# Whole 65-row blocks through DRAM, and weight loads issued by GpSimd, in a delta-rule attention and mixer kernel

## The chip, the cores and the metric

The kernel runs on one core of one Trainium2 chip. The metric is device time in microseconds (us) of the slowest core, so here of the only one. Each execution also has the mean clock granted to TensorE beside it. Timed medians are of repeated executions; stage lengths come from one profiled execution of each kernel, whose span is some 1.8 us shorter than the time of the same execution.

## The reference, cut to what matters

```python
# q, k, v: (4, 8, 768, 48); beta: (4, 8, 768)
for t in range(S):                                  # delta rule, 768 steps
    y[:, :, t] = einsum('bhd,bhde->bhe', q[:, :, t], state)
    v_old = einsum('bhde,bhd->bhe', state, kt)      # kt: normalized k
    state = state + bt * outer(kt, vt - v_old)
x = y.transpose(0, 2, 1, 3).reshape(4, 768, 384)
h  = maximum(x.transpose(0, 2, 1) @ w_tok1, 0) @ w_tok2    # token mixer
u  = x + h.transpose(0, 2, 1)
out = u + maximum(u @ w_ch1, 0) @ w_ch2                    # channel mixer
```

The four weight matrices arrive as 64-bit floats. The kernel takes them apart with integer operations and rounds them itself.

## The kernel before

Time is cut into chunks of 128 steps, six for each of the four sequences, 24 in all. Within a chunk, a 64×64 unit triangular matrix must be inverted for each head and half chunk. The kernel inverts the two 32×32 diagonal blocks of each matrix and makes the rest by matmuls. The inversions of up to four chunks (a "round": two chunks in round 0, four in each later one but the last) are done at once on VectorE, one block in each partition; to get there, masked blocks pass through DRAM and come back with another partition layout, and so does the inverse W.

```python
# prep(u), its end: the four 32x32 quarters of the masked blocks go to DRAM
for par in range(2):
    for i in range(2):
        lo = (4 * j + 2 * par + i) * NB
        row = C * par + HB * i                        # C = 64, HB = 32
        nc.sync.dma_start(
            out=xins[rnd][lo : lo + NB].rearrange("b s t -> s b t"),
            in_=gm[row : row + HB, :, 2, HB * i : HB * i + HB])

# invert(rnd): one block a partition, 60 dependent VectorE instructions
nc.sync.dma_start(out=x, in_=xins.pop(rnd)[0:n])
for s in range(1, HB - 1):
    nc.vector.tensor_tensor(out=tmp, in0=x[...], in1=x[...], op=ALU.mult)   # cut
    nc.vector.tensor_tensor(out=x[...], in0=x[...], in1=tmp, op=ALU.add)    # cut
nc.sync.dma_start(out=w_dram[0:n], in_=x)

# fetch_w(u): four 32-row DMAs bring W of a chunk back    (cut)

# round_weights: one piece of up to 128x384 float64, three VectorE instructions
d64 = loads.tile([128, WP], mybir.dt.int64, name="d64", bufs=3)[:, 0:n]
nc.sync.dma_start(out=d64, in_=src)
...
nc.vector.tensor_scalar(out=f, in0=hi, ...)
nc.vector.scalar_tensor_tensor(out=f, in0=hi, ...)
nc.gpsimd.tensor_tensor(out=f, in0=f, in1=lo, op=ALU.add)
yield
nc.vector.scalar_tensor_tensor(out=dst, in0=a, ..., in1=f.bitcast(FP32), ...)

# the plan: at(time, step, function): a scheduler fixes each engine's order from it
at(-2.7, 2.0 / (HB + 2), invert, 0)
at(-3.9, 0.25, load_weights, (w1, moe_w_tok1), (w2, moe_w_tok2))
at(2.5, 0.3, load_weights, (wc1, moe_w_ch1))
at(6.0, 0.05, load_weights, (wc2, moe_w_ch2))
```

The order of instructions on each engine is fixed when the kernel is built, and each engine works through its own order. An early piece of rounding is therefore done early, whether the engine has time for it or not.

## Time and profile before

| | before |
|---|---|
| time, median (lowest to highest) | 851.56 us (849.85 to 853.35, 4 runs) |
| profiled span, mean granted clock | 850.4 us, 0.924 |
| TensorE (PE) / VectorE (DVE) / GpSimd (POOL) busy | 732.3 / 394.8 / 111.6 us |
| time until TensorE is full | 253 us, in seven stages A to G |
| the rest, H | 597.4 us, of which TensorE is busy 584.1 |

How to read it: TensorE's share is high because H is full. The prediction says what the stages A to G hold, and why the change must act there.

### The profile page before, as it was taken

To read this page: it belongs to the slowest core of one execution; us is meant where nothing else is said; L and a number is where in the kernel's file an instruction comes from. 1 tells how busy PE (TensorE), PEld (TensorE's weight loads), DVE (VectorE), ACT (ScalarE), POOL (GpSimd) and SP (SyncE) were. 2 spreads that over 40 slices of the span, in tenths; PEclk is the share of its full clock that TensorE was granted. 3 is DMA by queue.
4 is the path that set the end of the run, shared out by engine and by line. 5 is a ranking of instruction groups with operands and counts; after the bars stand their busy time and mean duration, and the time that the engine had idled before them with its cause. 6 is when DMAs were issued, how large, how long until landed. Compare 5 with 4: busy or idle time off the path is not lost.

```text
span 850.4 us, 13384 instructions
## 1 busy us (share of the span) xinstructions
PE 732.3 (86%) x5080; PEld 606.6 (71%) x5080; DVE 394.8 (46%) x1081; ACT 253.0 (30%) x596; POOL 111.6 (13%) x142
## 2 busy tenths in 40 slices
PE   5630654969689999999999899999999999999998
PEld 4620644856469797887787888886898888678876
DVE  4487775756973459333267323493229422010000
ACT  5430422744234522333231333311332222111110
POOL 4322112223430211002000001110000000000000
PEclk9765755987899999999999999999999999999999
DMA  7763414445433441224122223202110200000000
GB/s 137 138 144 63 107 28 126 71 82 155 121 109 53 71 94 24 68 44 78 29 48 54 43 49 69 46 19 53 22 39 20 44 11 10 9 1 20 11 9 19
DMA packets 164591, 49.73 MB, mean 58 GB/s; under 512 B 155536, under 2 KB 158608, under 8 KB 164528
## 3 DMA queue, kind: packets, MB, share of 16 engines
q1 hardware_dynamic: 164480, 48.79, 26.6%
q8 instruction: 40, 0.66, 0.3%
q14 instruction: 23, 0.19, 0.1%
q10 hardware_dynamic: 48, 0.10, 0.0%
HBM read 37.85 MB, written 11.01 MB: 57 GB/s over the span
## 4 chain that ended last, share of the span: by engine, by line
PE 49%; DVE 9%; DMA 2%; ACT 2%; issue 1%; SPq 1%; ACTq 0%
PE p_c L549 16%; PE p_o L564 15%; DVE x L377 3%; DVE sub L373 3%; PE p_h L523 3%; PE p_s L482 2%; PE p_g L338 2%; PE p_q L453 2%; PE p L510 2%; PE p_w L470 2%; PE p_x L422 1%; PE p_z L413 1%; SPq L251 1%; PE p_ut L533 1%; DMA kst<-in_k_dram 1%
## 5 line engine op out<-in xcount | busy, mean ns | idle before, releaser
L549 PE MATMUL p_c<-u_t,wc 128*128 128x128 f32 x1728 | 218.2, 280 | 2.5 <-ACT u_t L537 1.8
L549 PEld LDWEIGHTS p_c<-u_t,wc 128*128 128x128 f32 x1728 | 206.5, 195 | 7.8 <-ACT u_t L537 2.5
L564 PE MATMUL p_o<-wc,r 128*128 128x384 f32 x576 | 197.5, 490 | 3.1 <-DVE wc L195 3.1
L564 PEld LDWEIGHTS p_o<-wc,r 128*128 128x128 f32 x576 | 105.0, 191 | 64.8 <-DVE wc L195 4.4
L556 ACT ACTIVATE r<-p_c 128x512 f32<-128x512 f32 x72 | 43.0, 597 | 156.8 <-PE p_c L549 156.4
L373 DVE TENSOR_TENSOR sub<-x 128x84 f32<-128x84 f32 (+22 forms) x210 | 77.3, 368 | 22.9 <-DMA x<-n_dram 18.3
L377 DVE TENSOR_TENSOR x<-x,sub 128x84 f32<-128x84 f32 (+22 forms) x210 | 76.7, 365 | 4.7
L338 PE MATMUL p_g<-kqt,kbd 128*128 128x128 f32 x384 | 60.1, 313 | 17.9 <-ACT kqt L326 17.7
L413 PE MATMUL p_z<-t,gm 128*65 128x64 f32 x384 | 30.7, 236 | 50.2 <-DVE t L407 49.8
L338 PEld LDWEIGHTS p_g<-kqt,kbd 128*128 128x128 f32 x384 | 55.1, 223 | 24.0 <-ACT kqt L326 22.5
L570 DVE TENSOR_TENSOR xb<-xb,p_o 128x384 f32<-128x384 f32 x24 | 13.3, 554 | 116.2 <-PE p_o L564 116.0
L413 PEld LDWEIGHTS p_z<-t,gm 128*65 128x65 f32 x384 | 28.7, 151 | 52.7 <-issue 28.5
L486 DVE TENSOR_TENSOR s_bd<-s_bd,p_s 64x192 f32<-64x192 f32 (+1 forms) x100 | 31.6, 316 | 73.9 <-PE p_s L482 72.2
L482 PE MATMUL p_s<-w_bd,gm 128*128 128x96 f32 x384 | 58.5, 297 | 5.2 <-ACT w_bd L474 4.9
L482 PEld LDWEIGHTS p_s<-w_bd,gm 128*128 128x128 f32 x384 | 52.6, 208 | 10.3 <-ACT w_bd L474 9.1
L340 DVE TENSOR_TENSOR gm<-p_g,mb 128x512 f32<-128x512 f32 x48 | 33.0, 690 | 57.3 <-PE p_g L338 55.0
L453 PE MATMUL p_q<-s_bd,kqt 128*128 128x96 f32 x352 | 50.9, 287 | 4.2 <-DVE s_bd L486 3.9
L453 PEld LDWEIGHTS p_q<-s_bd,kqt 128*128 128x128 f32 x352 | 47.1, 201 | 9.6 <-issue 3.0
L470 PE MATMUL p_w<-r_bd,wt 128*65 128x96 f32 x384 | 45.5, 263 | 7.2 <-issue 3.5
L455 DVE TENSOR_TENSOR r_bd<-v_st,p_q 64x192 f32<-64x192 f32 (+1 forms) x110 | 34.8, 316 | 35.1 <-PE p_q L453 23.0
L459 ACT ACTIVATE xb<-p_q 64x384 f32<-64x384 f32 (+1 forms) x55 | 23.0, 419 | 92.7 <-DVE r_bd L455 92.4
L474 ACT COPY w_bd<-p_w 64x192 f32<-64x192 f32 (+1 forms) x120 | 33.5, 280 | 54.0 <-PE p_w L470 52.0
(70 smaller groups left out, 708.8 us busy)
## 6 DMA issues: line engine op xcount, KB each, us to landing
d<-in_moe_w_ch_dram SPq DMA_DIRECT2D x24, 384.0 KB, 3.3
kpad<-in_k_dram SPq DMA_DIRECT2D x24, 192.0 KB, 3.5
kst<-in_k_dram SPq DMA_DIRECT2D x96, 48.0 KB, 2.6
qpad<-in_q_dram SPq DMA_DIRECT2D x24, 192.0 KB, 3.6
v_st<-in_v_dram SPq DMA_DIRECT2D x96, 48.0 KB, 2.6
out_dram<-xb SPq DMA_DIRECT2D x24, 192.0 KB, 1.9
n_dram<-gm SPq DMA_DIRECT2D x96, 32.0 KB, 1.7
wt<-w_dram SPq DMA_DIRECT2D x96, 32.0 KB, 2.1
```

The lines of the kernel that those rows point to most:

```text
L338: nc.tensor.matmul(p_g[:, i], kbd[:, nb], kqt[:, nb])
L373: nc.vector.tensor_tensor(out=tmp, in0=x[:, 0:s, s : s + 1].to_broadcast([n, s, w]), in1=x[:, s : s + 1, s + 1 : HB].to_broadcast([n, s, w ...
L377: nc.vector.tensor_tensor(out=x[:, 0:s, s + 1 : HB], in0=x[:, 0:s, s + 1 : HB], in1=tmp, op=ALU.add,)
L413: nc.tensor.matmul(p_z[0:65, nb], gm[:, lo : lo + 65], t11[:, nb])
L453: nc.tensor.matmul(p_q[:, p], kqt[:, 2 * p + cc], s0[:, p])
L455: nc.vector.tensor_tensor(out=r_bd[r, hp, e], in0=v_st[r, hp, cc], in1=p_q[hi, hp, e], op=ALU.subtract,)
L470: nc.tensor.matmul(p_w[0 : C + 1, p], wts[u % NW][:, w_lo : w_lo + C + 1], r_bd[:, p])
L474: nc.scalar.copy(w_bd[r, hp, e], p_w[lo, hp, e])
L482: nc.tensor.matmul(p_s[:, p], gm[:, 2 * p + cc, 0:2], w_bd[:, p])
L549: nc.tensor.matmul(p_c[:, i], wc1[:, cb, f * 128 : (f + 1) * 128], u_t[:, cb], start=(cb == 0), stop=(cb == NCB - 1),)
L556: nc.scalar.activation(r, p_c, ACTF.Relu)
L564: nc.tensor.matmul(p_o, r2[f // FG][:, f % FG], wc2[:, f], start=(f == 0), stop=(f == NHT - 1),)
```

## The change

The intent: fewer and longer transfers on the sync queue. The masked blocks are stored whole (64×64, with one spare row each, 65 rows of pitch). At that pitch the second diagonal 32×32 block lies exactly half a pitch after the first, so one strided transfer takes all diagonal blocks of a round. W is fetched as whole blocks, which needs zeros in the other quarters, so the two W buffers are cleared once. The 34 weight loads leave the sync queue for GpSimd. Smaller parts: three `kst` buffers and not two, the square in place, and some shifted plan times.

```diff
-        nc.sync.dma_start(out=d64, in_=src)
+        nc.gpsimd.dma_start(out=d64, in_=src)
...
-        nc.scalar.square(a, hi.bitcast(FP32))
+        a = hi.bitcast(FP32)                       # after both uses of hi
+        nc.scalar.square(a, a)
...
+    BP = C * C + C
+    def clear_w(i):                                # zeros over one W buffer
+        nc.gpsimd.dma_start(out=w_drams[i]..., in_=z.to_broadcast([128, n, 520]))
+    def diagonal(t, n):
+        t = t[0 : n * BP // 2].rearrange("(b x) -> b x", x=BP // 2)
+        return t[:, 0 : HB * C].rearrange("b (s t) -> b s t", t=C)[:, :, 0:HB]
...
-        ksts[u] = kst = loads.tile([128, NP, 2, D], FP32, name="kst")
+        ksts[u] = kst = loads.tile([128, NP, 2, D], FP32, name="kst", bufs=NK)
...
-        (four stores of 32-row quarters)
+            nc.sync.dma_start(out=rows(n_drams[rnd % 2], j, par), in_=gm[r, :, 2])
...
-        nc.sync.dma_start(out=x, in_=xins.pop(rnd)[0:n])
+        nc.sync.dma_start(out=x, in_=diagonal(n_drams[rnd % 2], n))
...
-        nc.sync.dma_start(out=w_dram[0:n], in_=x)
+        nc.sync.dma_start(out=diagonal(w_drams[rnd % 2], n), in_=x)
...
-        (four fetches of 32-row quarters)
+            nc.sync.dma_start(out=wt_of(u)[r], in_=rows(w_drams[rnd % 2], j, par))
...
+    for i in range(2):
+        at(-3.0 + i, 0, clear_w, i)
-                at(-2.7 + 0.4 * j, 0.06, prep, u)      # round 1
+                at(-3.0 + 0.4 * j, 0.06, prep, u)
-            at(-2.7, 2.0 / (HB + 2), invert, rnd)      # round 0
+            at(-2.5, 2.0 / (HB + 2), invert, rnd)
```

More of the change, by code (lines that the diff above doesn't have):

```diff
@@ L181, in round_weights @@
         f = loads.tile([128, WP], U32, name="w_f")[:, 0:n]
-        a = loads.tile([128, WP], FP32, name="w_a")[:, 0:n]
         nc.scalar.activation(lo, lo, ACTF.Copy, scale=2.0**-29)
-        nc.scalar.square(a, hi.bitcast(FP32))
         nc.vector.tensor_scalar(
@@ L218, with rows @@
     ksts = {}
-    xins = {}
-    xouts = {}
+    BP = C * C + C
+    n_drams, w_drams = [
+        [dram.tile([RU * 2 * NB * BP], FP32, name=f"{name}{i}") for i in range(2)]
+        for name in ("n_dram", "w_dram")
+    ]
+    def clear_w(i):
+        z = zst[:, None, 0:520]
+        n = w_drams[i].shape[0] // (128 * 520)
+        nc.gpsimd.dma_start(
+            out=w_drams[i].rearrange("(p n x) -> p n x", p=128, x=520),
+            in_=z.to_broadcast([128, n, 520]),
+        )
+    def diagonal(t, n):
+        t = t[0 : n * BP // 2].rearrange("(b x) -> b x", x=BP // 2)
+        return t[:, 0 : HB * C].rearrange("b (s t) -> b s t", t=C)[:, :, 0:HB]
+    def rows(t, j, par):
+        lo = (2 * j + par) * NB * BP
+        t = t[lo : lo + NB * BP].rearrange("(b x) -> b x", x=BP)
+        return t[:, 0 : C * C].rearrange("b (s t) -> s b t", t=C)
     rounds = [[0, 1], [2, 3, 4, 5]]
@@ L349, in prep @@
         rnd, j = round_of[u]
-        if j == 0:
-            xins[rnd] = dram.tile([RU * 4 * NB, HB, HB], FP32, name="n_dram")
         for par in range(2):
-            for i in range(2):
-                lo = (4 * j + 2 * par + i) * NB
-                row = C * par + HB * i
-                nc.sync.dma_start(
-                    out=xins[rnd][lo : lo + NB].rearrange("b s t -> s b t"),
-                    in_=gm[row : row + HB, :, 2, HB * i : HB * i + HB],
-                )
+            r = slice(C * par, C * par + C)
+            nc.sync.dma_start(out=rows(n_drams[rnd % 2], j, par), in_=gm[r, :, 2])
         yield
@@ L382, in invert @@
         nc.vector.memset(x.rearrange("b s t -> b (s t)")[:, 0 :: HB + 1], 1.0)
-        xouts[rnd] = w_dram = dram.tile([RU * 4 * NB, HB, HB], FP32, name="w_dram")
-        nc.sync.dma_start(out=w_dram[0:n], in_=x)
+        nc.sync.dma_start(out=diagonal(w_drams[rnd % 2], n), in_=x)
         yield
@@ L389, in fetch_w @@
         rnd, j = round_of[u]
-        w_dram, wt = xouts[rnd], wt_of(u)
-        for i in range(2):
-            for par in range(2):
-                lo = (4 * j + 2 * par + i) * NB
-                row = C * par + HB * i
-                nc.sync.dma_start(
-                    out=wt[row : row + HB, :, HB * i : HB * i + HB],
-                    in_=w_dram[lo : lo + NB].rearrange("b s t -> s b t"),
-                )
+        for par in range(2):
+            r = slice(C * par, C * par + C)
+            nc.sync.dma_start(out=wt_of(u)[r], in_=rows(w_drams[rnd % 2], j, par))
     def join(u):
@@ L602, in start @@
         return u if b == 0 else NCH * b + 0.4 + c * (NCH - 0.5) / NCH
-    for u in range(NK):
+    at(-9.5, 0, load_kq, 0)
+    at(-9.4, 5.6, load_beta)
+    for u in range(1, NK):
         at(-9 + 0.1 * u, 0, load_kq, u)
-    at(-8.95, 4, load_beta)
+    for i in range(2):
+        at(-3.0 + i, 0, clear_w, i)
     for rnd, us in enumerate(rounds):
@@ L610 @@
             if rnd == 0:
-                at(-3.5 + 0.3 * j, 0.06, prep, u)
+                at(-3.7 + 0.3 * j, 0.06, prep, u)
             elif rnd == 1:
-                at(-2.7 + 0.4 * j, 0.06, prep, u)
+                at(-3.0 + 0.4 * j, 0.06, prep, u)
             else:
```

## The prediction

> **What bounds the kernel now.** I read the page first, then cut the span into stages and asked for busy time by engine in each, then the same for the weight-rounding tile alone, then the timelines of VectorE, TensorE and the DMA queue at the seams.
>
> ```profile
> PE 732.3 (86%) x5080; PEld 606.6 (71%) x5080; DVE 394.8 (46%) x1081; ACT 253.0 (30%) x596; POOL 111.6 (13%) x142
> ...
> PE   5630654969689999999999899999999999999998
> ...
> PEclk9765755987899999999999999999999999999999
> ```
>
> TensorE is full from the twelfth slice (about 253 us) to the end. Before that it is half idle and its clock sags. The change can pay only in the first 253 us, unless it makes new holes later. The stages (bounds from the timeline: VectorE's first and last step of the first two triangular inversions, first matmul of the first mixer, TensorE full):
>
> ```profile
> core 0: us, PE busy (x) PEld busy (x) DVE busy (x) ACT busy (x) POOL busy (x), PEclk, DMA share, GB/s
> ...
> 8.60:48.40 39.80, 25.36 (x124) 22.32 (x124) 19.70 (x54) 21.61 (x48) 13.88 (x16) 0.79 0.76 145
> 48.40:78.70 30.30, 3.71 (x16) 3.48 (x16) 28.95 (x83) 5.60 (x12) 6.09 (x7) 0.58 0.47 96
> 78.70:87.80 9.10, 2.01 (x17) 1.88 (x17) 2.66 (x7) 0.93 (x3) 3.00 (x6) 0.50 0.64 136
> 87.80:131.40 43.60, 23.34 (x144) 20.26 (x144) 35.54 (x117) 14.70 (x44) 8.24 (x8) 0.62 0.27 67
> 131.40:139.30 7.90, 0.03 (x1) 0.03 (x1) 6.21 (x18) 2.05 (x5) 3.17 (x3) 0.50 0.57 133
> 139.30:202.20 62.90, 51.16 (x408) 47.03 (x409) 35.54 (x109) 32.22 (x92) 12.01 (x13) 0.80 0.46 97
> 202.20:253.00 50.80, 38.78 (x155) 25.32 (x155) 44.85 (x120) 17.51 (x37) 20.90 (x20) 0.90 0.40 120
> 253.00:850.40 597.40, 584.11 (x4169) 482.92 (x4167) 218.76 (x566) 156.53 (x353) 38.27 (x45) 1.00 0.18 38
> ```
>
> I call them A (preparing the masked blocks), B (inversion of round 0), C (its trip through DRAM), D (inversion of round 1, with the recurrence of round 0 between its steps), E (trip of round 1), F (recurrence of round 1), G (first mixer) and H. They are one chain: x has one buffer, so D cannot load before B has written out; F needs D's W; G needs F's rows. VectorE bounds B (28.95 of 30.30) and G (44.85 of 50.80). H has 13.3 us of TensorE idle; the rest of it is matmul.
>
> Weight rounding alone, by stage (columns: stage, VectorE, GpSimd, clock, DMA):
>
> ```profile
> 48.40:78.70 30.30, 5.29 (x13) 4.01 (x4) 0.58 0.47 96
> ...
> 139.30:202.20 62.90, 4.71 (x10) 3.53 (x4) 0.80 0.46 97
> 202.20:253.00 50.80, 23.35 (x44) 17.50 (x15) 0.90 0.40 120
> ```
>
> So 44 of the 102 VectorE rounding instructions (34 pieces of three) lie in G, which they make VectorE-bound.
>
> **What the Trainium skill says.** SBUF — State Buffer, section Who interferes with whom: a VectorE instruction with two SBUF inputs contends with a GpSimd one that reads SBUF, and the later one blocks. The trace agrees. GpSimd's rounding add runs at 65.72 for 1.00, and the inversion step issued after it takes three times its usual 0.39:
>
> ```profile
> 65.42 0.39 DVE L373 TENSOR_TENSOR sub<-x 64x234 f32<-64x234 f32 x1
> 65.83 1.14 DVE L377 TENSOR_TENSOR x<-x,sub 64x234 f32<-64x234 f32 x1
> ```
>
> Each piece rounded inside an inversion thus costs VectorE its three slots (0.27+0.47+0.47 us from start to start at 384 columns) and about 0.75 us of blocking. DMA: Bandwidth & Descriptors, section Issuing engines are not separate DMA queues: another issuing engine saves only sequencer time. In section Latency and other measured facts it gives the GpSimd path about 1 us to the first byte against 0.6; no run of before shows it, GpSimd issues nothing there. Its section Why small descriptors are slow has a fixed cost per piece. The trace agrees:
>
> ```profile
> kpad<-in_k_dram SPq DMA_DIRECT2D x24, 192.0 KB, 3.5
> kst<-in_k_dram SPq DMA_DIRECT2D x96, 48.0 KB, 2.6
> ...
> x<-n_dram SPq DMA_DIRECT2D x5, 512.0 KB, 4.3
> w_dram<-x SPq DMA_DIRECT2D x5, 512.0 KB, 2.6
> ```
>
> kpad is 1024 runs of 192 bytes, 64 for each of 16 engines, kst 256, 16 each: 0.9 us over 48 runs is 19 ns a run.
>
> **The change part by part.**
>
> *Queue.* n_dram and wt go from 96 issues each to 48 (runs of 256 bytes in place of 128); 34 weight loads leave the queue. That is 130 issues of 0.33 to 0.5 us, some 55 us of queue time over the span. It matters in A, where the queue issues almost without a pause to 67 us. The read of x for round 0, issued at 34.86, should go out near 29: six sets of k and q at 4 us, three stores of 1.1, from 0.74 on. But VectorE starts B only at 48.37, behind other work, so those 6 us are no gain by themselves. Three kst buffers and not two take a 3 us wait (180.8 to 183.9) off the queue in F, just ahead of the W load that TensorE waits 6.24 us for at 190.7.
>
> *DRAM trips.* x was 4 KB runs; it becomes 32 rows of 128 bytes out of a 256-byte pitch: 4096 runs, 256 an engine. At 19 ns the load goes from 4.3 to about 2.3+4.9 = 7 us; the store from 2.6 to about 6, or 4 for round 0, which is half. wt stays near 2.5.
>
> *Order.* This I take from the order of instructions in the two builds. With weight loads on a queue of their own, weights arrive early and the scheduler puts their rounding wherever it sees VectorE room. VectorE rounding instructions: ahead of B 18 before, 36 after; between B's steps 11 and 39; in C 1 and 20; in D 11 and 7; in F 17 and 0; from the next inversion on 44 and 0. So G is freed, but the work goes into B, the other stage that VectorE bounds. B also now starts behind the blocks of all six chunks, not five.
>
> *Extra transfers.* Two clears of w_dram at 1.06 MB, in A or near it, where DMA is already at 0.76; at the 145 GB/s seen there each is about 7 us of all engines, though nothing needs them before B's end.
>
> Stage by stage (after minus before, us):
> - A: a chunk's preparation repeats each 6.4 us (VectorE's second mask product at 23.06, 29.55, 35.83). Six chunks end near 16.9+5*6.4 = 49, plus the four rounding slots before B; GpSimd now has 12 adds, 14 issues at about 1 us (estimate from the page's first-byte figure) and the mask products, close to all of A. I take a start at 54: +5.5.
> - B: its own 60 steps are 21 us alone. Something between each step hides about 0.1 us of dependence, so some 16.5. 39 slots at 0.40 are 15.7, 13 blockings at 0.75 are 10, the other small ones 2.3: 45 with a little waiting 46. The same sum for before is 18.3+4.4+3+3 = 29, measured 30.3. Change +16.
> - C: store 4, W of the first chunk 1, load 7, waits: 13 to 15, with seven pieces in it, each limited by three buffers (issue 1, landing 3.3, rounding 2.5, so 7 us for three, 2.3 a piece, 16 for seven). I take 14.5: +5.5.
> - D: four fewer slots, W further ahead: -2.5.
> - E: +1.
> - F: 17 slots (6.8 us) gone, about half on its path, and half of the W wait: -7.
> - G: 44 rounding instructions gone. What remains on VectorE is about 22 us, so TensorE bounds it: 38.8 busy, a little less at a better clock, plus 3 of waits, 41: -10.
> - H: same matmuls; 3 us longer each way for x and W in five rounds against a freer queue: 0 to +3.
>
> Sum 5.5+16+5.5-2.5+1-7-10+1 = +9.5. A shorter G and a better-fed F would look like success; B pays for them.
>
> **The rivals.** (1) *The weights ride free in A to C and only G's gain counts.* Speaking for it: B's steps depend on each other, so a slot between them hides 0.1 us, and the queue in A is relieved. Against: B is at 96% VectorE already. It would give 851-17-3 = about 831. (2) *GpSimd becomes the brake:* issue, clears and adds in one in-order engine; the mask products of A stand behind loads that wait for a buffer held until the last rounding step (the square is now in place in d64). If each issue costs 2 us and not 1, A and B lose another 10 to 15: 870 to 878. (3) *The finer runs of x open holes in H:* five rounds at up to 6 us, 865 to 880; against it, TensorE has mixer matmuls to fill most of them: in H it idles only 13.3 us though each round's trip takes some 6 us.
>
> **Range and chances.** The sum gives 861. The savings in F and G are surer than the loss in A, where I may be too pessimistic, so I go down to 857. Rival 1 sets the lower side, 2 and 3 the upper: 841 to 875. Faster by 2% needs under 834.5: 0.12. Slower by 2% needs over 868.5: 0.22.
>
> **What would show it.** B's first to last step about 46 us with rounding steps between (under 35: wrong). D starting near 112 to 115 and not 87.8. No rounding in G, and G near 41. The x load near 7 us. GpSimd busy time rising only by its issues. H with 13 to 17 us of TensorE idle. The prediction is wrong if rounding beside an inversion costs under 1 us a piece, or if GpSimd's issues take several us.

## The result, and the profile after

| | before | after |
|---|---|---|
| time, median (lowest to highest) | 851.56 us (849.85 to 853.35) | 876.83 us (875.47 to 878.46, 4 runs) |
| profiled span, clock | 850.4 us, 0.924 | 873.7 us, 0.904 |

The ratio is 1.030 (95% interval 1.027 to 1.033): slower by 3%. Ratios here are of fast runs in the same rounds, so they are not quite the ratio of the medians quoted. Where two experiments are compared that ran in different rounds, I subtract their ratios to before and multiply by 851.5 us; each ratio has an interval of about ±0.3%, that is ±2.5 us, and the difference of two about ±3.5 us.

The page of after begins as follows: busy time by engine, then the busy tenths of TensorE, its granted clock and DMA in 40 slices.

```profile
PE 727.5 (83%) x5080; PEld 604.4 (69%) x5080; DVE 397.2 (45%) x1081; ACT 255.8 (29%) x596; POOL 131.1 (15%) x178
...
PE   5620016369699999999999999999999999999998
...
PEclk9755556569699999999999999999999999999999
DMA  9995281235513543233231414223111200000000
```

The amounts of work are almost those of before. GpSimd has 36 more entries and 20 us more (34 issues and two clears, some 0.56 us each). But slices 4 to 6, roughly 66 to 131 us, hold almost no TensorE work, and its clock falls to half there. DMA is full for the first three slices. The same row of before:

```profile
DMA  7763414445433441224122223202110200000000
```

The stages of after, cut at the same events, A to H (window, then its length, then busy time and count of PE, PEld, DVE, ACT and POOL, granted clock, DMA share and rate):

```profile
8.60:61.02 52.42, 28.23 (x140) 24.11 (x140) 33.35 (x78) 28.26 (x63) 30.56 (x38) 0.73 1.06 242
61.02:108.79 47.77, 0.00 (x0) 0.00 (x0) 46.39 (x113) 16.26 (x33) 26.77 (x34) 0.50 0.46 124
108.79:127.36 18.57, 1.62 (x15) 1.66 (x16) 10.95 (x22) 6.17 (x12) 9.58 (x13) 0.50 0.87 180
127.36:171.43 44.07, 25.28 (x148) 21.93 (x146) 34.41 (x118) 13.76 (x43) 6.85 (x8) 0.58 0.16 35
171.43:181.11 9.68, 0.00 (x0) 0.00 (x0) 0.87 (x2) 0.00 (x0) 0.00 (x0) 0.50 0.61 112
181.11:242.04 60.93, 51.42 (x408) 47.44 (x409) 31.55 (x103) 27.71 (x83) 9.75 (x12) 0.81 0.47 81
242.04:276.25 34.21, 33.64 (x151) 22.59 (x150) 23.73 (x73) 4.85 (x10) 1.73 (x2) 0.97 0.23 41
276.25:873.70 597.45, 583.51 (x4171) 483.26 (x4170) 212.77 (x564) 156.26 (x352) 38.63 (x45) 1.00 0.22 44
```

Lengths against the fence of stages in the prediction: A +12.6, B +17.5, C +9.5, D +0.5, E +1.8, F −2.0, G −16.6, H 0.0; together +23.3, the difference of the spans. The time was lost before the first inversion's trip through DRAM was over (A to C, +39.6) and only part of it came back in G. In B, VectorE is busy 46.39 of 47.77 us with 113 instructions, where before had 83. The weight-rounding tile alone, in A, B and C of after (columns VectorE, GpSimd, clock, DMA share, GB/s), shows what the extra instructions are:

```profile
8.60:61.02 52.42, 21.37 (x36) 10.52 (x12) 0.73 1.06 242
61.02:108.79 47.77, 23.43 (x41) 14.18 (x13) 0.50 0.46 124
108.79:127.36 18.57, 10.18 (x20) 6.37 (x6) 0.50 0.87 180
```

(The 41 of B include two that touch its edges; 39 lie between its steps.) In G the tile no longer appears. The timeline of VectorE in B of after shows how the two kinds of work alternate (start, duration, engine, line, operation):

```profile
62.15 0.20 DVE L392 TENSOR_TENSOR sub<-x 64x58 f32<-64x58 f32 x1
62.39 1.25 DVE L396 TENSOR_TENSOR x<-x,sub 64x58 f32<-64x58 f32 x1
63.57 0.34 DVE L183 TENSOR_SCALAR w_f<-d 128x384 uint32<-128x384 uint32 x1
63.84 0.23 DVE L392 TENSOR_TENSOR sub<-x 64x84 f32<-64x84 f32 x1
63.99 0.55 DVE L187 SCALAR_TENSOR_TENSOR w_f<-d,w_f 128x384 uint32<-128x384 uint32 x1
64.46 0.23 DVE L396 TENSOR_TENSOR x<-x,sub 64x84 f32<-64x84 f32 x1
```

A rounding step stands between two steps of an inversion again and again, and one `x<-x,sub` of 58 columns takes 1.25 us where its neighbour of 84 columns takes 0.23. GpSimd's rounding add runs at the same moment:

```profile
62.53 1.03 POOL L193 TENSOR_TENSOR w_f<-w_f,d 128x384 uint32<-128x384 uint32 x1
```

Each of the 13 adds in B overlaps one VectorE instruction that is stretched, to between 0.8 and 1.4 us; six of these are rounding steps themselves. In 11 of the 13 the stretched one had started after the add, as the prediction says. In two, this one among them, it had started up to 0.14 us before, so the start times alone do not decide who waits.

The transfers concerned, after, in the view of DMA issues (count, KB each, median us from issue to landing):

```profile
d<-in_moe_w_ch_dram POOLq DMA_DIRECT2D x24, 384.0 KB, 3.8
n_dram<-gm SPq DMA_DIRECT2D x48, 128.0 KB, 2.7
wt<-w_dram SPq DMA_DIRECT2D x48, 128.0 KB, 3.4
x<-n_dram SPq DMA_DIRECT2D x5, 512.0 KB, 6.0
w_dram<-x SPq DMA_DIRECT2D x5, 512.0 KB, 5.0
```

The x load went from 4.3 to 6.0 us and its store from 2.6 to 5.0 (before's in the prediction). The stores of masked blocks took 1.7 us before and now 2.7, the W fetches 2.1 and now 3.4: half as many, each with four times the bytes and twice the rows.

### The profile page after: what moved, and what is told of

The parts are those of the page before. It is cut to its first block, busy times and chain, and to the rows that moved or that the text cites. A ratio compares the mean times of both kernels' runs of the same rounds, so it can differ in the third digit from the quotient of the medians.

```text
span 873.7 us, 13277 instructions
## 1 busy us (share of the span) xinstructions
PE 727.5 (83%) x5080; PEld 604.4 (69%) x5080; DVE 397.2 (45%) x1081; ACT 255.8 (29%) x596; POOL 131.1 (15%) x178
## 5 line engine op out<-in xcount | busy, mean ns | idle before, releaser
L561 PE MATMUL p_c<-u_t,wc 128*128 128x128 f32 x1728 | 214.7, 277 | 1.2 <-ACT u_t L549 1.1
L561 PEld LDWEIGHTS p_c<-u_t,wc 128*128 128x128 f32 x1728 | 203.0, 192 | 5.0 <-ACT u_t L549 1.8
L576 PE MATMUL p_o<-wc,r 128*128 128x384 f32 x576 | 194.9, 487 | 0.0
L425 PE MATMUL p_z<-t,gm 128*65 128x64 f32 x384 | 32.6, 243 | 96.3 <-DVE t L419 96.3
L392 DVE TENSOR_TENSOR sub<-x 128x84 f32<-128x84 f32 (+22 forms) x210 | 75.9, 362 | 22.6 <-DMA x<-n_dram 17.6
L396 DVE TENSOR_TENSOR x<-x,sub 128x84 f32<-128x84 f32 (+22 forms) x210 | 74.6, 355 | 4.6
L364 PE MATMUL p_g<-kqt,kbd 128*128 128x128 f32 x384 | 58.6, 307 | 15.3 <-ACT kqt L352 15.2
L582 DVE TENSOR_TENSOR xb<-xb,p_o 128x384 f32<-128x384 f32 x24 | 13.3, 554 | 119.8 <-PE p_o L576 119.6
L364 PEld LDWEIGHTS p_g<-kqt,kbd 128*128 128x128 f32 x384 | 53.5, 217 | 20.4 <-ACT kqt L352 18.6
L465 PEld LDWEIGHTS p_q<-s_bd,kqt 128*128 128x128 f32 x352 | 47.9, 203 | 11.2 <-PE p_q L465 2.4
L353 POOL TENSOR_TENSOR gm<-kst,cs 128x384 f32<-128x384 f32 x24 | 21.1, 877 | 215.3 <-PE p_s L494 173.3
L482 PE MATMUL p_w<-r_bd,wt 128*65 128x96 f32 x384 | 45.3, 262 | 7.7 <-DVE r_bd L467 5.7
```

The source lines that it names most:

```text
L364: nc.tensor.matmul(p_g[:, i], kbd[:, nb], kqt[:, nb])
L392: nc.vector.tensor_tensor(out=tmp, in0=x[:, 0:s, s : s + 1].to_broadcast([n, s, w]), in1=x[:, s : s + 1, s + 1 : HB].to_broadcast([n, s, w ...
L396: nc.vector.tensor_tensor(out=x[:, 0:s, s + 1 : HB], in0=x[:, 0:s, s + 1 : HB], in1=tmp, op=ALU.add,)
L425: nc.tensor.matmul(p_z[0:65, nb], gm[:, lo : lo + 65], t11[:, nb])
L465: nc.tensor.matmul(p_q[:, p], kqt[:, 2 * p + cc], s0[:, p])
L482: nc.tensor.matmul(p_w[0 : C + 1, p], wts[u % NW][:, w_lo : w_lo + C + 1], r_bd[:, p])
```

## The experiments

My theory after reading the traces: the one word `gpsimd` costs most of it, through the order. Weights arrive early, their rounding goes into the stage that VectorE bounds, and it costs more there than it saves in G. Rivals: the DRAM layout and its extra traffic; GpSimd as a brake.

Stage lengths of all runs in us, with the VectorE rounding instructions in A / B / C / D / E and F together / G and later, and the ratio to before. The last two counts are parted at the first step of the next inversion, a few instructions before the end of F:

| run | ratio | A | B | C | D | E | F | G | H | rounding |
|---|---|---|---|---|---|---|---|---|---|---|
| before | 1 | 39.8 | 30.3 | 9.1 | 43.6 | 7.9 | 62.9 | 50.8 | 597.4 | 18/11/1/11/17/44 |
| after | 1.0297 | 52.4 | 47.8 | 18.6 | 44.1 | 9.7 | 60.9 | 34.2 | 597.5 | 36/39/20/7/0/0 |
| e1 after, sync weights | 1.0040 | 45.0 | 27.0 | 11.5 | 44.2 | 10.6 | 61.8 | 48.7 | 596.4 | 18/9/3/8/20/44 |
| e2 before, GpSimd weights | 1.0122 | 40.3 | 52.8 | 15.3 | 41.6 | 5.6 | 61.8 | 39.7 | 593.8 | 33/44/18/7/0/0 |
| e3 after, no clear, quarter fetch | 1.0221 | 53.6 | 45.8 | 18.4 | 40.8 | 8.5 | 60.8 | 34.7 | 595.5 | 40/38/21/3/0/0 |
| e4 after, gated | 1.0055 | 46.1 | 22.6 | 13.4 | 40.0 | 9.7 | 74.4 | 40.6 | 597.2 | 30/0/2/1/36/33 |
| e5 after, no GpSimd add | 1.0113 | 46.9 | 41.2 | 18.5 | 42.0 | 9.4 | 61.2 | 34.4 | 596.8 | 38/39/21/4/0/0 |
| e6 before, small parts | 0.9970 | 45.6 | 27.1 | 8.9 | 46.2 | 7.2 | 61.4 | 52.7 | 591.4 | 18/9/3/11/15/46 |
| e7 before, gated | 0.9891 | 37.0 | 25.3 | 11.4 | 40.9 | 5.4 | 70.2 | 40.6 | 604.6 | 30/0/2/1/41/28 |
| e8 before, gated a round later | 0.9905 | 37.7 | 25.4 | 9.0 | 39.5 | 5.4 | 72.7 | 41.6 | 601.0 | 30/0/0/0/49/23 |
| e9 e6 + GpSimd weights | 1.0104 | 47.8 | 47.9 | 15.1 | 45.3 | 5.6 | 56.8 | 39.6 | 590.7 | 37/39/16/10/0/0 |
| e10 e9 + gate | 0.9879 | 45.5 | 22.6 | 11.4 | 40.1 | 5.6 | 69.4 | 40.5 | 598.5 | 30/0/2/1/36/33 |
| e11 e3 with the clears | 1.0251 | 53.6 | 47.7 | 18.6 | 42.8 | 8.2 | 60.8 | 33.9 | 596.4 | 36/39/20/7/0/0 |
| e12 e4, no clear, quarter fetch | 0.9994 | 44.3 | 22.7 | 15.7 | 39.0 | 8.5 | 73.2 | 40.6 | 596.8 | 30/0/3/0/37/32 |

G begins with the first mixer matmul and ends with the first 24 output matmuls. As other work is mixed in on both sides, a few us can move across these borders, so F, G and H are also read as a sum. Each row of stages is one execution, and those of a kernel differ by 1 to 8 us (e7 and e10, among others, were profiled in their slowest, 846.0 and 844.1).

**e1: the one word undone, in after.**

```diff
-        nc.gpsimd.dma_start(out=d64, in_=src)
+        nc.sync.dma_start(out=d64, in_=src)
```

> The changed kernel with one word put back: the weight pieces are issued by the sync queue again. In the build this returns the rounding to where it was (18, 9, 3, 8, 20, 44 of the 102 instructions in A, B, C, D, F and later). Theory 1, the early rounding is what costs: A to C shrink to near the old lengths (B 30 us, not 47.8) and the time falls to 846 to 858. Theory 2, the whole-block DRAM traffic (clears, 128-byte runs) is what costs: B shrinks, but A stays above 48 and the trips long, and the time stays at 866 or more.

Measured: 854.62 us, ratio 1.0040 (1.0014 to 1.0066). Some 22 of the 25 us are gone. The window of B, with 9 rounding instructions left in it:

```profile
53.65:80.68 27.03, 0.00 (x0) 0.00 (x0) 25.41 (x74) 3.79 (x8) 3.03 (x3) 0.52 0.33 68
```

So with the weights on the sync queue everything else in the change costs little.

**e2: that word alone, in before.**

```diff
-        nc.sync.dma_start(out=d64, in_=src)
+        nc.gpsimd.dma_start(out=d64, in_=src)
```

> The kernel before with that one word changed alone: weight pieces issued by GpSimd, all DRAM traffic as before, no clears. The build has 33, 44, 18, 7, 0, 0 rounding instructions by stage. Theory 1: 864 to 878, B near 48, C near 15 to 18. Theory 2: 846 to 856. If the two causes add, about 866, with A several us shorter than in the changed kernel since there are no clears.

Measured: 861.09 us, ratio 1.0122 (1.0093 to 1.0151). The trace shows the prediction's pattern in full: 44 rounding instructions inside B, none from E on, B +22.5, C +6.2, G −11.1.

```profile
48.93:101.76 52.83, 3.58 (x16) 3.40 (x16) 49.80 (x124) 17.90 (x38) 33.06 (x39) 0.53 0.63 152
```

The time lies between the two forecasts, below the first theory's 864. The word alone costs about 10 us, yet undoing it in after gains 22. The two parts of the change do not add, and e6 and e9 to e12 look for the difference.

**e3: after without the clears, W fetched by quarters.**

```diff
-    for i in range(2):
-        at(-3.0 + i, 0, clear_w, i)
...
-            nc.sync.dma_start(out=wt_of(u)[r], in_=rows(w_drams[rnd % 2], j, par))
+            for i in range(2):                     # src = rows(...), row = C*par + HB*i
+                e = slice(HB * i, HB * i + HB)
+                nc.sync.dma_start(out=wt[row : row + HB, :, e], in_=src[e, :, e])
```

> The changed kernel without the two clears: W's 32-row quarters alone are fetched out of the pitched blocks (96 issues again), weights still by GpSimd. If the clears fill the DMA engines in A and so delay it, A falls from 52.4 to about 45 and the time to 866 to 870. If A is long only because of the rounding in it, the time stays within 2 us of 876.8. B stays near 47 in both.

Measured: 868.65 us, ratio 1.0221 (1.018 to 1.0262), 0.76% or 6.5 us better than after. A did not shorten (53.6), against the thought that the clears crowd it; the time came out as that thought had it, so the forecast was missed in part.

**e4: after, with the 24 channel-weight pieces held back.** A one-element copy on GpSimd, which reads the first W of round 0 once it is back, stands ahead of the first three loads; the rest queue behind.

```diff
+        if gate is not None:                       # gate = lambda: wts[0]
+            nc.gpsimd.tensor_copy(out=d64.bitcast(FP32)[0:1, 0:1], in_=gate()[0:1, 0:1])
         nc.gpsimd.dma_start(out=d64, in_=src)
```

> The changed kernel, the 24 channel weight pieces held back until the first W is joined (a one-element copy ahead of the first three loads), still issued by GpSimd. The build has 30, 0, 2, 1, 36, 33 rounding instructions by stage. Theory 1: B falls to about 25 us and C to 10 to 13, A to about 47 to 50, F a little longer, time 835 to 852. If it is GpSimd's way of issuing that costs, and not the order, the time stays above 865.

Measured: 855.59 us, ratio 1.0055 (1.003 to 1.008). That is 3.6 us above the forecast's 852. The run keeps GpSimd issue and the layout, and moves the 24 loads with their rounding. Its B and its F:

```profile
54.69:77.29 22.60, 0.00 (x0) 0.00 (x0) 20.67 (x66) 1.14 (x3) 2.51 (x5) 0.55 0.21 38
...
140.37:214.81 74.44, 52.54 (x409) 47.85 (x409) 54.36 (x141) 41.76 (x112) 32.02 (x42) 0.78 0.64 146
```

B without any rounding is 22.6 us, so in after each of the 39 instructions cost (47.8 − 22.6)/39 = 0.65 us. This is an upper figure: B of after has 47 VectorE instructions more (113 against 66), and over all of them it is 0.54. The gate takes the loads' own traffic out of B as well; but VectorE is busy there for 46.39 of 47.77 us in after, and waits less than 1 us for weights. F took 36 (with E; 39 up to its end) and grew by (74.4 − 60.9)/36 = 0.37 us for each. From before to after, F and G together lost 61 of them and 18.6 us, 0.30 each, the layout's part in F and G included. An instruction moved from there into B therefore costs 0.54 to 0.65 and saves 0.3 to 0.4. This shows the exchange of the prediction, with its rates.

**e5: after without GpSimd's rounding add.** The add was taken out, so the last bits of the low word are lost.

```diff
-        nc.gpsimd.tensor_tensor(out=f, in0=f, in1=lo, op=ALU.add)
```

> The changed kernel without GpSimd's rounding add, so that the low bits of the weights are cut off (wrong in the last place on purpose). The order keeps 38, 39, 21, 4, 0, 0 rounding instructions by stage, so all of VectorE's slots stay where they are. If blocking by GpSimd's reads is 0.75 us a piece as predicted, B falls by 13 x 0.75 = 10 us to about 38, A and C by some 4 each as there is no add to wait for, and the time to 856 to 864. If the early rounding costs its VectorE slots alone, B stays above 45 and the time above 870.

Measured: 860.83 us, ratio 1.0113 (1.0086 to 1.0141), some 16 us better than after, with nearly the same order (39 instructions in B). Its B:

```profile
55.46:96.68 41.22, 0.00 (x0) 0.00 (x0) 37.07 (x112) 16.27 (x33) 12.50 (x21) 0.51 0.60 164
```

B fell by 6.6 us, 0.5 us for each of 13 adds (10 had been expected), and A by 5.6; C did not fall. VectorE's busy time in B fell by 9.3 us with one instruction fewer, 0.72 for each add, so the loss lay inside its instructions; the rest returned as waits. Removing the add also frees GpSimd, and the order ahead of B is another one, without the wait of 3.67 us that is shown further down, so not all of the 16 us is blocking.

**e6: only the small parts, in before** (plan times of after, three `kst` buffers, square in place).

```diff
-            at(-2.7, 2.0 / (HB + 2), invert, rnd)
+            at(-2.5, 2.0 / (HB + 2), invert, rnd)      # and the other plan times
+        ... name="kst", bufs=NK)    a = hi.bitcast(FP32); nc.scalar.square(a, a)
```

> The kernel before with only the small parts of the change: new plan times, three kst buffers, the square in place; weights on the sync queue, DRAM traffic as before. The weights-on-sync version of the changed kernel measured 854.62, 3.4 us over before. If that was the finer DRAM runs (C and E longer by 2.4 and 2.7), this one is at 848 to 853 with E near 8 and C near 9. If the later start of B (A 45 and not 39.8) was from the plan times, A is again near 44 to 45, and it may be at 854.

Measured: 848.81 us, ratio 0.9970 (0.994 to 0.9999). A grows by 5.8 (more chunks are prepared ahead of B), B, F and H shrink. A long A is not itself a loss if the work it holds is taken from later stages.

**e7 and e8: before with GpSimd loads and the gate**, on the first W of round 0 (e7) or of round 1 (e8: `wts[2]`).

```diff
-        nc.sync.dma_start(out=d64, in_=src)
+        if gate is not None:                       # e7: wts[0]    e8: wts[2]
+            nc.gpsimd.tensor_copy(out=d64.bitcast(FP32)[0:1, 0:1], in_=gate()[0:1, 0:1])
+        nc.gpsimd.dma_start(out=d64, in_=src)
```

> The kernel before, weights issued by GpSimd, the 24 channel pieces held back until the first W is joined; DRAM traffic as before. 30, 0, 2, 1, 41, 28 rounding instructions by stage. Like the gated version of the changed kernel (A 46.1, B 22.6, C 13.4, D 40.0, E 9.7, F 74.4, G 40.6) but with the short trips and with A as in the version with GpSimd's issue alone (40.3, two mask products left to B): A 41, B 25, C 10, D 40, E 6 to 7, F 74, G 40, H 595: about 841 to 847, faster than before. If the finer runs cost nothing, it equals 855.6.

> The same with the pieces held back until the first W of round 1 is joined, so that D and E hold no rounding at all: 30, 0, 0, 0, 49, 23. Rounding in F costs about 0.37 us an instruction (74.4 against 60.9 with 36 of them), so F about 78 and G 38: 839 to 848, within 3 us of the other gate. If rounding in F beyond what VectorE has free there delays the recurrence more than that, F exceeds 82 and the time 850.

Measured: 841.36 us, ratio 0.9891 (0.985 to 0.9932), and 842.88 us, 0.9905 (0.9881 to 0.9929). With the rounding kept out of B, GpSimd issue turns from a loss of 1.2% into a gain of 1%. Where in F it lands makes no difference that these runs resolve.

**e9: small parts and GpSimd issue together, in before.**

```diff
+        (e6, and)
-        nc.sync.dma_start(out=d64, in_=src)
+        nc.gpsimd.dma_start(out=d64, in_=src)
```

> The kernel before with GpSimd's issue and the small parts (plan times, three kst buffers, square in place), DRAM traffic as before. Apart they measured +9.9 and -2.4, so 858 to 860 if they add. The changed kernel measured 876.8; if it is the DRAM traffic together with GpSimd's early loads that fills the DMA engines in A, this one stays at 858 to 862 with A plus B near 93. If instead the plan times with the early rounding make A long (B behind six chunks), it is at 868 or more with A plus B near 99.

Measured: 859.73 us, ratio 1.0104 (1.0067 to 1.0141). They simply add (−0.3% and +1.2% against +1.0%), so the missing piece between e9 and after, 1.93% or 16.4 us, belongs to the DRAM layout. By stages, after minus e9: A +4.6, C and E +7.6, F, G and H together +5.5, B and D −1.3; sum 16.4 (from the table's rounded lengths; the spans differ by 16.3). A and B together take 95.8, where 93 had been expected.

**e10: e9 with the gate** (e9's diff and e7's gate on `wts[0]`).

```diff
+        (e9, and) nc.gpsimd.tensor_copy(out=d64..., in_=wts[0][0:1, 0:1]) ahead of the first 3 loads
```

> The gated kernel of 841.36 (pieces held back until the first W is joined, DRAM as before) with the small parts added. 30, 0, 2, 1, 36, 33 rounding instructions by stage, the same as the gated changed kernel at 855.59. If the small parts are worth their 2.4 here too: 838 to 840. The distance to 855.59 is then the DRAM change alone, in a kernel whose order is the same: 14 to 18 if it costs as much as beside early weights, 6 as with weights on the sync queue.

Measured: 840.04 us (839.58 to 844.1), ratio 0.9879 (0.9848 to 0.9911): the fastest median here, and it beats both kernels, with the old layout. Against e9 only the place of the 24 loads and their rounding differs: 2.25%, 19 us. From after to e4 the same gate gave 2.42%. Its E and F:

```profile
128.24:133.81 5.57, 0.00 (x0) 0.00 (x0) 0.87 (x3) 0.00 (x0) 0.00 (x0) 0.50 0.38 118
133.81:203.22 69.41, 51.18 (x409) 46.69 (x409) 50.81 (x138) 41.08 (x110) 31.72 (x40) 0.80 0.60 142
```

e4 has the same places for the rounding and the new layout: its E is 9.7 and its F 74.4. The ratios put the layout at 1.76%, 15.0 us, here (10.3 between the two profiled executions, which are e4's fastest and e10's slowest). With sync weights (e1 against e6) it is 0.70%, 6.0 us.

**e11: e3 with the clears put back**, which parts them from the fetch.

```diff
+    for i in range(2):
+        at(-3.0 + i, 0, clear_w, i)
```

> The changed kernel with the clears but the quarter fetch of W (the version without either measured 868.65, the changed kernel 876.83). If the clears cost the 8 us, this one is at 875 to 878; if fetching W as whole blocks costs them, it is at 867 to 870.

Measured: 872.80 us, ratio 1.0251 (1.0223 to 1.0278), between the two forecasts. Clears +0.30% (2.6 us) and whole-block fetch +0.46% (3.9 us), each within the error of such a difference; together the 6.5 us of e3.

**e12: e4 without clears, W by quarters** (e3's diff on e4).

```diff
-        at(-3.0 + i, 0, clear_w, i)
+        (quarter fetch as in e3)
```

> The gated changed kernel took 855.6 us and the gated kernel with the old DRAM layout 840.0, so the layout costs 15.6 us here. This run takes the two clears away and fetches W by 32-row quarters again, and keeps the 65-row pitch and the diagonal transfers of x. In the ungated form the clears were worth 4.1 us and the whole-block fetch 4.0. If these two simply add: 847 us (845 to 850), trip E near 8.3 us in place of 9.7, and the recurrence F shorter by some 2 of its 5 extra us. If instead the layout's cost lies in the diagonal runs alone, and the clears only hurt where weight loads crowd them in the first stage: 852 to 856. If clears and fetch explain it all: 840 to 843.

Measured: 850.66 us, ratio 0.9994 (0.9967 to 1.0021), just past the first theory's 845 to 850 and below the second's 852. Clears and fetch are worth 0.61% or 5.2 us here, like the 6.5 ungated. What then remains of the layout (whole-block stores, diagonal transfers of x) is 1.15%, 9.8 us, against 1.17%, 10.0 us ungated (e3 against e9). So two thirds of its cost beside GpSimd loads lies in these, in both orders. The medians in the issue view give the trip of round 1 some 5 us more (load 1.7, store 2.4, the stores ahead of it 1.0) and that of round 0, at half the size, some 3 (load 4.7 and 5.5, store 2.9 and 4.1, the stores ahead 1.0). This estimate of 8 us comes near the 10, and was not tested by itself.

## Why the prediction was right or wrong

The direction, the mechanism and the pattern of stages were right; the size was not. 876.8 lies just above the range (841 to 875). Its sum was +9.5; the spans differ by +23.3. Here each term meets its stage. The way from before to after by e6 (small parts), e9 (and GpSimd issue) and after (and the layout) tells the cause.

- **B, +16: right (+17.5).** Own steps 22.6 and not 21. For a rounded piece the prediction had three slots of 0.40 and 0.75 of blocking, 1.95 us; measured 3 × 0.65 = 1.94, which has the other small instructions in it that the prediction counted apart (2.3 us). So near a match is in part luck. Blocking took 0.72 us an add of VectorE's busy time (e5), as said; only 0.5 of it came off the stage when the add went.
- **A, +5.5: failed (+12.6).** The six chunks ahead of B were named, and e6 shows them: +5.8, all of what was predicted. On top come +2.2 with GpSimd's issues and +4.6 with the layout, which the prediction put at nothing there. Most of the 4.6 is one wait. VectorE starts a like rounding step at 56.12 in after and at 56.16 in e9. In e9 the first step of the inversion comes next:

```profile
56.16 0.35 DVE L183 TENSOR_SCALAR w_f<-d 128x384 uint32<-128x384 uint32 x1
56.43 0.18 DVE L373 TENSOR_TENSOR sub<-x 64x30 f32<-64x30 f32 x1
```

In the built order of after one more rounding step stands ahead of it, and VectorE waits 3.67 us for that step's weights:

```profile
56.51 0.56 DVE L187 SCALAR_TENSOR_TENSOR w_f<-d,w_f 128x384 uint32<-128x384 uint32 x1
60.74 0.36 DVE L183 TENSOR_SCALAR w_f<-d 128x384 uint32<-128x384 uint32 x1 [3.67 <-DMA d<-in_moe_w_ch_dram]
61.02 0.17 DVE L392 TENSOR_TENSOR sub<-x 64x30 f32<-64x30 f32 x1
```

GpSimd issued the load waited for at 55.33. In e9 the load issued at 55.37 is met between two inversion steps, with a wait of 0.69 us. e3 and e11, whose A is 53.6, have the wait ahead of B too, 2.67 and 2.43 us. In e4 and e10 the last mask product stands just ahead of B and no weights do, and the layout's part in A is +0.6. No run took the wait away by itself. The read of x, expected near 29 us, went out at 36.43 (before 34.86), with DMA full in A (share 1.06, before 0.76) and the four `kst` issues of a chunk at 2.6 to 4.6 us (2.6 to 3.4 before); but it was issued 24 us before B began and did not set A's end.
- **C, +5.5: half the size (+9.5).** GpSimd issue gives +6.2 of it, as 16 to 20 rounding instructions fall into the stage, and the layout +3.5. The lengths of the transfers were near: 4 for the store and 7 for the load, and in C of after they took 4.5 and 7.3. But they do not set its end. The load, issued at 114.59, had landed by 121.9, and D's first step came at 127.36, behind rounding steps of which one waited 3.08 us for its weights. That is the prediction's other sum (16 for seven pieces), from which it went down to 14.5.
- **D, −2.5: wrong (+0.5), as a sum of two.** Four rounding instructions fewer are worth what was said: e2 has 7 in D and 41.6 us, before 11 and 43.6. The plan times, left out of this term, lengthen it (e6, 11 and 46.2); after with its 7 has 44.1.
- **E, +1: right (+1.8), as a sum of two.** Without rounding in it and with the old layout E is 5.6; the layout adds 4.1.
- **F, −7, and G, −10: right in the sum (−17; measured −18.6), wrong in the split (−2.0 and −16.6).** With the old layout F does fall by 6.1 (e9, 56.8): TensorE's wait for W in it is 1.6 us, and was 6.2. The layout puts 4.1 back. VectorE no longer bounds G (23.73 of 34.21); TensorE does, with 33.64, less than the 38.8 assumed, at a better clock and because the borders moved.
- **H, 0 to +3: right (0.0).** TensorE idles 13.9 us in it and idled 13.3 (e9 also 13.3). The finer runs opened no holes, so rival 3 fell.
- **Going from 861 down to 857: wrong.** The reason given was that A might be too pessimistic. A was the term most underrated, by 7 us; C by 4 and D by 3 come next, and these three are the miss of 13.8.

Rival 1 (weights ride free, 831) is refuted by the 0.65 us in B. Rival 2 came out near the measured number, 870 to 878, for the wrong reason: it wanted 2 us an issue, and the trace has 0.54 to 0.73; and mask products that stand behind loads did not hold up A, where VectorE waits 1.1 us for GpSimd in after and 6.0 in before.

The step that failed, then, is the layout's price, and with it A, C and D. Its terms gave C and E a few us, H up to 3, and A nothing; in A the order that came with it left VectorE waiting 3.67 us for weights just ahead of B. It measured 16.4 us in this kernel and 15.0 in the gated one. The rest of the loss, 10 to 11 us, is the net of moving the rounding by GpSimd issue (+1.2% in e2, +1.3% from e6 to e9). That exchange was predicted; its net was not given apart from the layout's, as the term of C mixes the two.

Still open: why the layout costs 15 to 16 us beside GpSimd loads and only 6 beside sync loads. The exposed trips do not tell the cases apart: C and E together grow by 6.0 us (sync), 6.1 (gated) and 7.6 (ungated). Nor are the transfers longer beside GpSimd loads: the x load has a median of 6.0 us in after, 5.8 in e4 and 6.4 in e1. The differences lie in A (−0.6, +0.6, +4.6, the last mostly the wait shown) and in F, G and H (+1.4, +3.7, +5.5). One thought: with weights on the sync queue, the 96 issues that the layout saves there speed the weights as well, and this gain is gone once GpSimd issues them. No run took that by itself.

## What to carry to other kernels

A change that only moves a load to another queue can move the work behind the load: look at the built order of the engine that uses the data, and count how many of its instructions land in a stage which that engine already bounds, and see what stands just ahead of that stage's first step. The same word cost 1.2% with one order and gained 1.1% with a one-element gate that held the loads back. Price longer strided trips in each stage that waits for one, and beside all else that shares the DMA engines there, not only where the chain shows them first.

## What the Trainium skill lacked or had wrong

- DMA: Bandwidth & Descriptors, section Issuing engines are not separate DMA queues: it says that another issuing engine only saves time on the sequencer. That section does not say that the data then also arrive at another time, nor that a fixed order may put the work on them elsewhere: 34 loads moved to GpSimd cost 1.2% (e2), and gained 1.1% with a gate (e7).
- The same page, section Latency and other measured facts: it has about 1 us to the first byte for the GpSimd path and 0.6 otherwise, but no time for which an issue holds GpSimd. That was 0.54 to 0.73 us here; I had taken the 1 us for it. The 128×384 channel-weight loads landed after 3.8 us and 3.3 before, which agrees with the page's difference in size.
- The same page, section Why small descriptors are slow: it gives a price in bus cycles a packet, from which the length of a transfer like these is not to be read. Going from 4 KB runs to 128 bytes at a pitch of 256, the 512 KB load rose from 4.3 to 6.0 us and the store from 2.6 to 5.0. With 248 more runs on each of 16 engines that is 7 and 10 ns a run, an estimate. The prediction's 19 ns was too much: it put the whole difference between `kpad` and `kst` down to the runs, though the two also differ in size (192 and 48 KB).
- SBUF — State Buffer, section Who interferes with whom: the blocking is there, but no size for such a pair (its two factors come from another measurement). For a 128×384 add on GpSimd between the steps of an inversion on VectorE it was 0.72 us of VectorE's busy time an add, and about 0.5 us of the stage (B 47.8 and 41.2, e5).
